# A scaled sum split into three pieces: early x quarters of an attention and MoE kernel

## The chip, the cores and the metric

The kernel runs on one core of one Trainium2 chip. The metric is the device time of one execution in microseconds (us). TensorE is called PE, VectorE DVE, ScalarE ACT, GpSimd POOL; SP only issues DMAs here. Each engine works through its own list of instructions in order and waits on semaphores for the others.

## The reference

Attention with a learned bias of relative positions, and after it a feed-forward pair of products whose input is the attention's output.

```
scores = scale * q @ k^T                       # batch 4, heads 8, seq 576, head_dim 64
x = (log1p(|i - j|) / log1p(max(i, 1)))[..., None]
scores += relu(x @ w1 + b1) @ w2               # a bias for every head
attn = exp(scores - max);  attn /= sum + 1e-9
a = attn @ v                                   # as 2304 tokens x 512
h = a @ w_in                                   # 512 x 2048
g = h where h >= 1, 0 where h <= -1, else (h + 1)^2 / 4
out = g @ w_out                                # 2048 x 512
```

## The kernel before, in words

Every fp32 product is made of products of numbers that are split into a high and a low part. So beside each product there are splits: a cast to the high part, and a subtraction for the low part.

There are three stages. Up to some 69 us the bias of all heads is computed and stored to DRAM. From there to some 345 us runs the attention, in 16 units n = 0 to 15 (a pair of heads and a batch each, some 17 us a unit). Then comes the feed-forward part (MoE).

A unit has five blocks of rows, k = 0 to 3 and L. A block makes two PSUM tiles of scores `S{n}_{k}_{j}` on PE (lines 455 and 456; the L block one tile, 476 and 477). DVE adds the bias, writes the result to SBUF as `e` and finds the row's extreme `mx` in one instruction (458, for L 478). ACT takes the exponential (465, 484). PE transposes `e` into PSUM tiles `T` (521, 526, 535), and these are split into `hi` and `lo` on ACT and DVE (496, 497), or by way of an ACT copy `c` (501) on DVE (505) or POOL (503) for `hi` and POOL (506) for `lo`. Then come the products with v on PE (559, 561), whose PSUM tiles `O` ACT copies out (562). They are stored to DRAM as `xT`, not yet divided by the sums of the rows; the reciprocals of these sums are stored as `rT`. PSUM has two buffers for all `S` tiles of the stage, so a score tile can start only when the tile two before it has been read by DVE: `S_3_1` waits for the read of `S_2_1`, `S_L` for the read of `S_3_0`.

For the next units the same engines cast k (163) and v (178) on DVE and make their low parts on POOL (136).

The MoE needs the attention's output as x, in quarters (k, j) of 128 x 384, multiplied by the reciprocals and split. Eight of these quarters, j = 0 and 1 of block 0, are made in the attention already, as soon as their tokens are complete. `load_x` asks for two halves of `xT` and for the reciprocals, and `split_x` (399) hands back three pieces: `scaled` (DVE: `scale_x`, the sum of the two halves at 396 and the product with the reciprocals at 397, each 128 x 384), `high` (ACT, 409) and `rest` (POOL, 413). `plan_x` (593) puts the load into half-step T and piece i into half-step T1 + i of a table `XQ`; a half-step is half a block, ten to a unit, so T1 = 43 is unit 4, half-step 3. The early quarters (0,0), (1,0) and (2,0) fall into units 4, 8 and 12; the other five into units 13 to 15. The home of a quarter is a buffer of another use: "raw" is also that of the next weights' load.

The order on an engine is partly pinned: what goes through `keep` stays in the program's order, the rest is placed by a scheduler when the kernel is built. The MoE makes its later x with `scale_x` itself.

Of the kernel before, what the change touches and what calls it, by code (L numbers as in the profile page):

```python
# [13 lines left out]
ALU = mybir.AluOpType  # L14
# [33 lines left out]
def attn_cpb_moe_kernel(ctx, tc, qk, vL, cb, win, wout, lw, ident, ii, out):  # L48
    nc = tc.nc
# [6 lines left out]
    TH = TB // 2  # L56
# [81 lines left out]
    def keep(ins):  # L138
        tc.keep_in_program_order(ins)

    def pool(ins):
        if KEEP and go[0]:
            tc.keep_in_program_order(ins)
# [213 lines left out]
    def x_tile(z, k, part, name):  # L357
        if z == 0:
            return xp0.tile([P, TH], F32R, tag=f"x{'hl'[part]}{k}", name=name)
        at = 2 * k + part  # L360
        g = min(at // 3, 2) + (at == 7)
        if at % 3 == 0 or at == 7:
            tag, w, n_ = ("qk", QW, CFG["rawb"][0]) if g < 2 else ("v", 10 * D, CFG["rawb"][1])
            room[g] = lp.tile([P, w], F32R, tag=tag, name=name, bufs=n_)
        c0 = TH * (at % 3 if at < 6 else 0)
        return room[g][:, c0 : c0 + TH]

    def load_x(blk, k, j, home="x"):

        src = xT[k][blk // TB][:, :, TH * j : TH * j + TH].rearrange("(s d) i c -> d s i c", s=2)  # L370
        rp = rps[0]
        if home != "raw":
            if home == "bias":
                r = bp.tile([P, 2 * S], F32, tag="bias", name=f"x{blk}_{k}_{j}").rearrange("p (a b) -> p a b", a=3)
            else:
                r = rp.tile([P, 3, TH], F32, tag="x", name=f"x{blk}_{k}_{j}", bufs=1)
            r, rr = r[:, 0:2], r[:, 2]
        else:
            r = rp.tile([P, 2 * DM], F32, tag="raw", name=f"x{blk}_{k}_{j}")[:, : 2 * TH].rearrange("p (a b) -> p a b", a=2)
            rr = rp.tile([P, DM], F32, tag="a", name=f"xr{blk}_{k}_{j}")[:, :TH]  # L380
        for i in range(2):
            nc.sync.dma_start(out=r[D * i : D * i + D], in_=src[:, :, i])
        c0 = blk + TH * j
        c1 = c0
        while c1 < c0 + TH:
            t = c1 % S
            e = min(c0 + TH, c1 - t + (512 if t < 512 else S))
            for i in range(2):
                at = 512 * i + t if t < 512 else 1024 + D * i + t - 512
                row = rT[k][c1 // S][at : at + e - c1].unsqueeze(0)  # L390
                nc.sync.dma_start(out=rr[D * i : D * i + D, c1 - c0 : e - c0], in_=row.to_broadcast((D, e - c1)))
            c1 = e
        return r, rr

    def scale_x(r, rr, out):
        keep(nc.vector.tensor_tensor(out=r[:, 0], in0=r[:, 0], in1=r[:, 1], op=ALU.add))
        keep(nc.vector.tensor_tensor(out=out, in0=r[:, 0], in1=rr, op=ALU.mult))

    def split_x(k, j, home):

        r, rr = load_x(0, k, j, home)
        x = r[:, 0]

        def scaled():
            scale_x(r, rr, x)

        def high():
            xs[k, j] = [x_tile(j, k, i, f"x{'hl'[i]}0_{k}_{j}") for i in range(2)]
            keep(nc.scalar.copy(xs[k, j][0], x))

        def rest():
            h, l = xs[k, j]
            pool(nc.gpsimd.tensor_tensor(out=l, in0=x, in1=h.bitcast(F32), op=ALU.subtract))

        return scaled, high, rest

    with ExitStack() as ph:
        tp1 = ph.enter_context(tc.tile_pool(name="a_eT1", bufs=1))
# [172 lines left out]
        def plan(T, f):  # L591
            jobs.setdefault(T, []).append(f)

        def plan_x(k, j):
            T, home, T1 = XQ[k, j]

            def load():
                assert all((k, t) in made for t in range(TH * j, TH * j + TH))
                for i, f in enumerate(split_x(k, j, home)):
                    plan(T1 + i, f)  # L600

            plan(T, load)
# [96 lines left out]
    with ExitStack() as ph:  # L699
# [232 lines left out]
        for blk in (0, TB):  # L932
            for m in range(2 * NF):
                f, j = m // 2, m % 2
# [4 lines left out]
                c = gp.tile([P, TH], F32, tag="c", name=f"c{blk}_{m}")  # L939
# [47 lines left out]
        for g in range(NG2):  # L987
            blk, f = b2, 2 * g
            for s_ in range(NS):
# [31 lines left out]
                else:  # L1021
                    fo, j = {2: (f, 0), 4: (f + 1, 1), 5: (f + 1, 0), 6: (f, 1)}[s_]
# [78 lines left out]
```

## Time and profile before

| | |
|---|---|
| time, median of 3 runs | 747.65 us (746.45 to 749.12) |
| the profiled execution's own time | 747.49 us |
| its span, first to last instruction | 745.7 us |
| PE busy | 701.6 us, 94% of the span |
| DVE, POOL, ACT busy | 541.5, 519.2, 516.4 us |
| mean granted PE clock | 0.992 |

The span is the stretch that the trace covers; the remaining 1.8 us lie around it. Busy shares are means over three stages that differ: what one place is worth is read in the rows of that place. A duration in the timeline can hold time in which an instruction had begun and was held up.

### The profile page before, as it was taken

To read this page: it belongs to the slowest core of one execution; us is meant where nothing else is said; L and a number is where in the kernel's file an instruction comes from. 1 tells how busy PE (TensorE), PEld (TensorE's weight loads), DVE (VectorE), ACT (ScalarE), POOL (GpSimd) and SP (SyncE) were. 2 spreads that over 40 slices of the span, in tenths; PEclk is the share of its full clock that TensorE was granted. 3 is DMA by queue.
4 is the path that set the end of the run, shared out by engine and by line. 5 is a ranking of instruction groups with operands and counts; after the bars stand their busy time and mean duration, and the time that the engine had idled before them with its cause. 6 is when DMAs were issued, how large, how long until landed. Compare 5 with 4: busy or idle time off the path is not lost. (4 is left out here: it accounts for less than half of the span.)

```text
span 745.7 us, 13716 instructions
## 1 busy us (share of the span) xinstructions
PE 701.6 (94%) x4640; PEld 620.3 (83%) x4640; DVE 541.5 (73%) x1047; ACT 516.4 (69%) x1151; POOL 519.2 (70%) x440
## 2 busy tenths in 40 slices
PE   5687999999999999999999999999999998999997
PEld 2234899998988889889988898898989987888896
DVE  7899888888898898886876866354465557666653
ACT  8896989888888889877565656444534446666563
POOL 8986777888878888852667677466655645666652
PEclk9999999999999999999999999999999999999999
DMA  8887799977997898634355554133021002000002
GB/s 231 239 268 227 200 250 244 305 204 183 263 234 196 201 256 205 156 113 147 113 177 162 189 155 138 43 96 75 1 65 32 1 4 82 1 1 1 0 1 85
DMA packets 58518, 103.37 MB, mean 139 GB/s; under 512 B 12480, under 2 KB 32464, under 8 KB 58448
## 3 DMA queue, kind: packets, MB, share of 16 engines
q1 hardware_dynamic: 56000, 92.44, 43.7%
q0 software_dynamic: 2304, 9.96, 6.4%
q8 instruction: 37, 0.61, 0.4%
q14 instruction: 33, 0.27, 0.1%
q10 hardware_dynamic: 144, 0.09, 0.1%
HBM read 67.38 MB, written 25.12 MB: 124 GB/s over the span
## 5 line engine op out<-in xcount | busy, mean ns | idle before, releaser
L951 POOL TENSOR_TENSOR gl<-c,gh 128x384 fp32r<-128x384 f32 x64 | 70.9, 1107 | 104.2 <-issue 86.8
L506 POOL TENSOR_TENSOR lo<-c,hi 128x512 fp32r<-128x512 f32 x75 | 101.5, 1369 | 29.7 <-DVE hi L505 27.1
L716 PE MATMUL y<-w1h,gl 128*128 128x512 f32 x288 | 114.0, 396 | 0.0
L716 PE MATMUL y<-w1l,gh 128*128 128x512 f32 x288 | 113.7, 395 | 0.0
L716 PE MATMUL y<-w1h,gh 128*128 128x512 f32 x288 | 112.0, 389 | 0.0
L465 ACT ACTIVATE e<-e,mx 128x576 f32<-128x576 f32 x128 | 100.6, 790 | 12.7 <-DVE mx L458 12.6
L458 DVE CUSTOM_DVE_ANT_0 e<-S,bias 128x576 f32<-128x576 f32 x128 | 94.3, 750 | 12.6 <-PE S L456 12.0
L455 PE MATMUL S<-kh,qa 128*128 128x288 f32 x256 | 78.4, 323 | 6.8 <-DVE mx L458 4.6
L769 ACT ACTIVATE c<-c,half_s 128x384 f32<-128x384 f32 x64 | 39.4, 616 | 60.7 <-DVE c L766 60.7
L456 PE MATMUL S<-ls,qa 128*128 128x288 f32 x256 | 72.3, 300 | 0.0
L521 PE MATMUL T<-id_s,e 128*128 128x128 f32 x512 | 70.7, 274 | 1.3 <-DVE lo L497 0.8
L977 POOL TENSOR_TENSOR gl<-c,gh 128x384 fp32r<-128x384 f32 x32 | 32.8, 1024 | 50.0 <-issue 23.3
L716 PEld LDWEIGHTS y<-w1h,gl 128*128 128x128 f32 x288 | 54.0, 187 | 11.6
L521 PEld LDWEIGHTS T<-id_s,e 128*128 128x128 f32 x512 | 58.7, 142 | 4.1 <-DVE lo L497 1.3
L284 ACT ACTIVATE u<-lw,nthr 128x576 f16<-128x576 f32 (+17 forms) x104 | 57.7, 644 | 5.1 <-PE B L303 2.7
L716 PEld LDWEIGHTS y<-w1l,gh 128*128 128x128 f32 x288 | 54.0, 187 | 8.0
L716 PEld LDWEIGHTS y<-w1h,gh 128*128 128x128 f32 x288 | 54.1, 188 | 7.7
L303 PEld LDWEIGHTS <-qh 128*32 128x32 f16 x704 | 19.1, 102 | 49.2 <-issue 21.2
L455 PEld LDWEIGHTS S<-kh,qa 128*128 128x128 f32 x256 | 48.2, 188 | 11.7 <-DVE mx L458 8.7
L772 DVE TENSOR_TENSOR c<-h,c 128x384 f32<-128x384 f32 x64 | 35.5, 554 | 26.8 <-ACT c L769 26.0
L286 POOL TENSOR_SCALAR u<-lw,thr 128x576 f16<-128x576 f32 (+17 forms) x36 | 51.5, 1442 | 4.3 <-PE B L303 3.1
L947 ACT CAST gh<-c 128x384 fp32r<-128x384 f32 x64 | 32.9, 513 | 30.7 <-DVE c L772 28.7
(264 smaller groups left out, 2117.5 us busy)
## 6 DMA issues: line engine op xcount, KB each, us to landing
bias_d<-y SPq DMA_DIRECT2D x36, 295.5 KB
qk<-in_qk_dram SPq DMA_DIRECT2D x16, 608.0 KB
qa<-in_qk_dram POOLq DMA_DIRECT2D x16, 608.0 KB, 7.0
x<-xT SPq DMA_DIRECT2D x48, 192.0 KB
raw<-in_win_dram SPq DMA_DIRECT2D x16, 512.0 KB
raw<-in_wout_dram SPq DMA_DIRECT2D x16, 512.0 KB
v<-in_vL_dram SPq DMA_DIRECT2D x16, 320.0 KB
qa<-ls SPq DMA_DIRECT2D x32, 152.0 KB
```

Source lines behind the costliest of these rows:

```text
L284: tc.keep_in_program_order(nc.scalar.activation(u[:, :n_], lw1[:, :n_], AF.Sigmoid, bias=nthr[:, m : m + 1], scale=STEEP))
L286: EN[x].tensor_scalar(out=u[:, :n_], in0=lw1[:, :n_], scalar1=thr[:, m : m + 1], scalar2=None, op0=ALU.is_gt)
L455: nc.tensor.matmul(ps[:, hf, :HS], qs[:, qc], kh[:, kc : kc + HS], start=True, stop=False)
L456: nc.tensor.matmul(ps[:, hf, :HS], q0[:, qc], kl[:, kc : kc + HS], start=False, stop=True)
L458: nc.vector.tensor_tensor_reduce(out=ev.rearrange("p (a b) -> p a b", a=2), in0=ps[:, :, :HS], in1=bias[k][:, S * j : S * j + S].rearrange ...
L465: lambda ev=ev, j=j: nc.scalar.activation(ev, ev, AF.Exp, bias=mx[:, j : j + 1], scale=-1.0, accum_out=sm[:, 4 * j + k : 4 * j + k + 1])
L506: r = nc.gpsimd.tensor_tensor(out=lo, in0=m, in1=hi.bitcast(F32), op=ALU.subtract)
L521: nc.tensor.transpose(ps[:, tb, :], e[:, c0 : c0 + P], id_s)
L716: a = nc.tensor.matmul(out, w, x, start=start, stop=stop)
L769: keep(nc.scalar.activation(c, c, AF.Square, scale=0.5, bias=half_s))
L772: keep(nc.vector.tensor_tensor(out=c, in0=h, in1=c, op=ALU.max))
L951: keep(nc.gpsimd.tensor_tensor(out=gl, in0=c, in1=gh.bitcast(F32), op=ALU.subtract))
```

## The change

The pieces of a quarter become five: the sum, the first half of the product (columns 0 to 191), its second half (192 to 383), the high part, the low part. For the quarters (0,0), (1,0) and (2,0) they stand in half-steps T1, T1 + 1, T1 + 2, T1 + 2, T1 + 3, in place of T1 (sum and product), T1 + 1, T1 + 2. For the other five the sum and both halves stay together in T1, and high and low part keep their half-steps.

```
-        def scaled():
-            scale_x(r, rr, x)
+        def summed():
+            keep(nc.vector.tensor_tensor(out=x, in0=x, in1=r[:, 1], op=ALU.add))
+
+        def scaled(i):
+            c = slice(TH // 2 * i, TH // 2 * i + TH // 2)
+            keep(nc.vector.tensor_tensor(out=x[:, c], in0=x[:, c], in1=rr[:, c], op=ALU.mult))
...
-        return scaled, high, rest
+        return summed, lambda: scaled(0), lambda: scaled(1), high, rest
...
-                for i, f in enumerate(split_x(k, j, home)):
+                for i, f in zip((0, 1, 2, 2, 3) if j == 0 and k < 3 else (0, 0, 0, 1, 2), split_x(k, j, home)):
                     plan(T1 + i, f)
```

What this does to the lists of the engines is shown at three places. First DVE in unit 4, before; x0_0_0 is the quarter, xr0_0_0 its reciprocals, vs5 the next unit's v, and the ISA rows are the reads of score tiles (e, mx):

```order
L396 TENSOR_TENSOR x0_0_0_2469<-x0_0_0_2469 128x384
L397 TENSOR_TENSOR x0_0_0_2469<-x0_0_0_2469,xr0_0_0_2470 128x384
L178 CAST vs5_2696<-v5_2515 128x10x64
L458 ISA e4_2_2609,mx4_2_2608<-S4_2_1_2616,bias1_2_2361 128x576
L458 ISA mx4_2_2608 128x1
L497 TENSOR_TENSOR lo4_0_2557<-T4_1_0_2627,hi4_0_2556 128x4x128
L497 TENSOR_TENSOR lo4_0_2557<-T4_1_1_2634,hi4_0_2556 128x4x128
L458 ISA e4_3_2649,mx4_3_2648<-S4_3_0_2650,bias1_3_2400 128x576
L458 ISA mx4_3_2648 128x1
L497 TENSOR_TENSOR lo4_0_2557<-T4_s0_2641,hi4_0_2556 128x256
L458 ISA e4_3_2649,mx4_3_2648<-S4_3_1_2656,bias1_3_2400 128x576
```

and now:

```order
L405 TENSOR_TENSOR x0_0_0_2469<-x0_0_0_2469 128x384
L178 CAST vs5_2697<-v5_2515 128x10x64
L462 ISA e4_2_2608,mx4_2_2607<-S4_2_1_2615,bias1_2_2361 128x576
L462 ISA mx4_2_2607 128x1
L409 TENSOR_TENSOR x0_0_0_2469<-x0_0_0_2469,xr0_0_0_2470 128x192
L501 TENSOR_TENSOR lo4_0_2557<-T4_1_0_2624,hi4_0_2556 128x4x128
L501 TENSOR_TENSOR lo4_0_2557<-T4_1_1_2631,hi4_0_2556 128x4x128
L462 ISA e4_3_2649,mx4_3_2648<-S4_3_0_2650,bias1_3_2400 128x576
L462 ISA mx4_3_2648 128x1
L501 TENSOR_TENSOR lo4_0_2557<-T4_s0_2638,hi4_0_2556 128x256
L409 TENSOR_TENSOR x0_0_0_2469<-x0_0_0_2469,xr0_0_0_2470 128x192
L462 ISA e4_3_2649,mx4_3_2648<-S4_3_1_2656,bias1_3_2400 128x576
```

The product has left the place between the sum and the cast of v; its first half stands behind the read of S4_2_1, its second half behind `lo` of T4_s0, ahead of the read of S4_3_1. Units 8 and 12 change in the same way.

Then ACT in the same unit, before; xh0_0_0 is the quarter's high part, c a copy of a transposed tile, x4_0 the copies of the products with v:

```order
L465 ACTIVATE e4_2_2609,sum4_2476<-e4_2_2609,mx4_2_2608 128x576
L409 CAST xh0_0_0_2624<-x0_0_0_2469 128x384
L496 CAST hi4_0_2556<-T4_s0_2641 128x256
L501 COPY c4_2669<-T4_2_0_2664 128x512
L501 COPY c4_2678<-T4_2_1_2673 128x512
L465 ACTIVATE e4_3_2649,sum4_2476<-e4_3_2649,mx4_3_2648 128x576 x2
L562 COPY x4_0_2698<-O4_0_0_2699 128x256
L484 ACTIVATE e4_L_2685,sum4_2476<-e4_L_2685,mx4_4_2684 128x576
L562 COPY x4_0_2698<-O4_0_1_2711 128x256
```

and now:

```order
L469 ACTIVATE e4_2_2608,sum4_2476<-e4_2_2608,mx4_2_2607 128x576
L500 CAST hi4_0_2556<-T4_s0_2638 128x256
L505 COPY c4_2670<-T4_2_0_2665 128x512
L505 COPY c4_2679<-T4_2_1_2674 128x512
L469 ACTIVATE e4_3_2649,sum4_2476<-e4_3_2649,mx4_3_2648 128x576
L413 CAST xh0_0_0_2645<-x0_0_0_2469 128x384
L469 ACTIVATE e4_3_2649,sum4_2476<-e4_3_2649,mx4_3_2648 128x576
L566 COPY x4_0_2699<-O4_0_0_2700 128x256
L566 COPY x4_0_2699<-O4_0_1_2712 128x256
L488 ACTIVATE e4_L_2686,sum4_2476<-e4_L_2686,mx4_4_2685 128x576
```

The high part of the quarter goes behind the first exponential of block 3, and the exponential of the L block goes behind the second copy x4_0. POOL's list is the same as before, so its low part of the quarter stands ahead of the same instructions as before.

Last DVE at quarter (3,0), in unit 14, before; lo13_1 are low parts of the unit before:

```order
L505 CAST hi13_1_4995<-T13_3_1_5105 128x4x128
L396 TENSOR_TENSOR x0_3_0_5017<-x0_3_0_5017 128x384
L497 TENSOR_TENSOR lo13_1_4996<-T13_L_5143,hi13_1_4995 128x4x64
L397 TENSOR_TENSOR x0_3_0_5017<-x0_3_0_5017 128x384
L497 TENSOR_TENSOR lo13_1_4996<-T13_s1_5152,hi13_1_4995 128x320
```

and now:

```order
L509 CAST hi13_1_4999<-T13_3_1_5109 128x4x128
L405 TENSOR_TENSOR x0_3_0_5021<-x0_3_0_5021 128x384
L501 TENSOR_TENSOR lo13_1_5000<-T13_L_5148,hi13_1_4999 128x4x64
L409 TENSOR_TENSOR x0_3_0_5021<-x0_3_0_5021 128x192 x2
L501 TENSOR_TENSOR lo13_1_5000<-T13_s1_5157,hi13_1_4999 128x320
```

One product has become two instructions next to each other, with nothing else moved. It is the same at (0,1), (1,1), (2,1) and (3,1).

## Rows read from the trace of the kernel before

**Rows 1.** Windows, 140 to 300 us: PE, PEld, DVE, ACT, POOL busy; clock, DMA

```profile
140.00:300.00 160.00, 150.95 (x1151) 143.23 (x1150) 140.84 (x305) 140.66 (x366) 132.52 (x110) 1.00 0.88 223
```

**Rows 2.** Timeline of PE: start, duration, line, operation, idle before it, its releaser

```profile
142.60 0.40 PE L455 MATMUL S<-kh,qa 128*128 128x288 f32 x1 [1.16 <-DVE mx L458]
211.86 0.40 PE L455 MATMUL S<-kh,qa 128*128 128x288 f32 x1 [1.54 <-DVE mx L458]
279.84 0.40 PE L455 MATMUL S<-kh,qa 128*128 128x288 f32 x1 [1.04 <-DVE mx L458]
```

**Rows 3.** Timeline of DVE in unit 12

```profile
276.56 1.73 DVE L397 TENSOR_TENSOR x<-x,xr 128x384 f32<-128x384 f32 x1
278.21 0.90 DVE L178 CAST vs<-v 128x640 fp32r<-128x640 f32 x1
279.03 0.74 DVE L458 CUSTOM_DVE_ANT_0 e<-S,bias 128x576 f32<-128x576 f32 x1
279.70 1.28 DVE L497 TENSOR_TENSOR lo<-T,hi 128x512 fp32r<-128x512 f32 x2
```

**Rows 4.** Timeline of POOL in unit 12

```profile
274.61 3.26 POOL L136 TENSOR_TENSOR ls<-qk,kh 128x608 fp32r<-128x608 f32 x2
277.81 0.95 POOL L503 CAST hi<-c 128x512 fp32r<-128x512 f32 x1
278.84 1.40 POOL L506 TENSOR_TENSOR lo<-c,hi 128x512 fp32r<-128x512 f32 x1
```

**Rows 5.** Timelines of DVE and POOL, instructions that no other one blocked

```profile
595.72 0.42 DVE L866 TENSOR_TENSOR sum_w<-sum_w,w 128x256 f32<-128x256 f32 x1
299.61 0.54 DVE L397 TENSOR_TENSOR x<-x 128x384 f32<-128x384 f32 x1
295.61 1.28 POOL L506 TENSOR_TENSOR lo<-c,hi 128x512 fp32r<-128x512 f32 x1
```

**Rows 6.** Timelines of DVE, POOL and PE at quarter (2,1), unit 15

```profile
324.25 1.64 DVE L397 TENSOR_TENSOR x<-x 128x384 f32<-128x384 f32 x1
324.20 1.28 POOL L506 TENSOR_TENSOR lo<-c,hi 128x512 fp32r<-128x512 f32 x1
326.77 0.82 PE L559 MATMUL O<-hi,vs 128*128 128x320 f32 x4 [1.59 <-DVE sum L672]
```

**Rows 7.** Timeline of PE in unit 12, start of S_L

```profile
281.71 0.40 PE L476 MATMUL S_L<-kh,qa 128*128 128x288 f32 x1
```

**Rows 8.** Timelines of DVE and POOL in unit 8

```profile
208.79 0.85 DVE L397 TENSOR_TENSOR x<-x,xr 128x384 f32<-128x384 f32 x1
211.73 1.28 DVE L497 TENSOR_TENSOR lo<-T,hi 128x512 fp32r<-128x512 f32 x2
209.31 1.48 POOL L506 TENSOR_TENSOR lo<-c,hi 128x512 fp32r<-128x512 f32 x1
```

**Rows 9.** Timelines of ACT and DVE behind unit 8: e_L, T_L

```profile
216.60 0.78 ACT L484 ACTIVATE e_L<-e_L,mx 128x576 f32<-128x576 f32 x1
221.19 0.37 ACT L496 CAST hi<-T_L 128x256 fp32r<-128x256 f32 x1
221.84 0.42 DVE L497 TENSOR_TENSOR lo<-T_L,hi 128x256 fp32r<-128x256 f32 x1
```

**Rows 10.** Timelines of DVE and POOL at quarter (0,1), unit 13

```profile
301.82 0.76 DVE L458 CUSTOM_DVE_ANT_0 e<-S,bias 128x576 f32<-128x576 f32 x1 [0.40 <-PE S L456]
299.76 1.55 POOL L506 TENSOR_TENSOR lo<-c,hi 128x512 fp32r<-128x512 f32 x1 [2.87 <-DVE hi L505]
```

**Rows 11.** Timelines of DVE, POOL and PE at quarter (3,0), unit 14

```profile
307.00 0.63 DVE L397 TENSOR_TENSOR x<-x 128x384 f32<-128x384 f32 x1
307.29 2.75 POOL L506 TENSOR_TENSOR lo<-c,hi 128x512 fp32r<-128x512 f32 x2
308.17 0.82 PE L559 MATMUL O<-hi,vs 128*128 128x320 f32 x4 [0.92 <-DVE lo L497]
```

**Rows 12.** Busy time and granted clock behind the wait at 326.77

```profile
329.00:331.00 2.00, 2.00 (x10) 2.00 (x9) 0.57 (x1) 1.94 (x5) 0.00 (x0) 0.50 0.70 198
```

## The prediction

> **What bounds the kernel now.** I read the page's busy shares first, then windows of the attention, then PE's waits there, and last the timelines of DVE, POOL and PE side by side around each early quarter. In the middle of the attention PE works 150.95 of 160 us, but DVE 140.84, ACT 140.66 and POOL 132.52 [rows 1]: PE is ahead by little, and what keeps it waiting is a chain on DVE here and there. Three of its longest waits there stand at the same place, `S_3_1` in units 4, 8 and 12, released by `mx`, the read of `S_2_1`: 1.16 + 1.54 + 1.04 = 3.74 us [rows 2]. That is all that the spreading of the first three quarters can win directly.
>
> Unit 12 shows why the read is late. The product begins at 276.56 and lasts 1.73 us [rows 3], where one that nothing blocks takes 0.54 [rows 5]. It ends at 278.29, that is 0.42 behind the end of POOL's pair `ls` (274.61 + 3.26 = 277.87) [rows 4]. The cast `vs` begins at 278.21 and ends at 279.11, 0.35 behind the end of POOL's `hi` (277.81 + 0.95 = 278.76); and POOL's next, `lo`, begun at 278.84, ends at 280.24, 1.13 behind the end of `vs` [rows 3, 4]. So a DVE instruction that takes all its operands from SBUF and a POOL instruction exclude each other. They take turns, one whole instruction each, although on DVE's list product and `vs` are neighbours. The read of `S_2_1` (279.03) waits behind both.
>
> **Prices.** A product of 384 columns costs 0.54, a DVE sum of 256 columns 0.42 [rows 5], so 0.001 a column, and a half of 192 some 0.36 us when free. Behind a block it needs 0.42 - 0.18 = 0.24 from the release. If POOL has an instruction ready when the first of two neighbouring halves ends, the second half waits for it: 1.13 for a `lo`. Two halves then end 0.24 + 1.13 + 0.24 - 0.42 = 1.19 us later than one product.
>
> The row shows `hi` between product and `vs` (278.29 to 278.76) although both DVE instructions were ready [rows 3, 4]. The Trainium skill ("SBUF — State Buffer", section "SBUF: two separate sides") says of the pair of ports that DVE and GpSimd share that it is "an exclusive lock, not a bandwidth split", held for the whole instruction. By that rule every added instruction boundary gives POOL one more turn, which speaks against cutting a product in two; if a lock outlasted the boundary, the two halves would cost about what the product does. The trace agrees with the page.
>
> **Units 4, 8 and 12.** In unit 12 the sum stays as it is. `vs` follows it and waits for the pair `ls` until 277.87, so it ends at 278.22, 0.89 before 279.11; the read of `S_2_1` starts at 278.14 and `S_3_1` at 279.84 - 0.89 = 278.95. Most of its wait goes. What is late next is `S_L`, which needs the read of `S_3_0`, and that stands on DVE behind first half, `lo`, `lo`. Before, it started at 281.71 [rows 7].
>
> The first half starts 0.67 behind the read (279.03 to 279.70 in [rows 3]), at 278.81. POOL, freed by `vs` at 278.22, makes `hi` (0.47, as 278.29 to 278.76) and starts `lo` 0.08 later, at 278.76 or 278.77 [rows 4]. The two ask for the port within 0.05 us. The trace has this very race at quarter (2,1): POOL's `lo` started at 324.20, DVE's product at 324.25, and the product took 1.64 and ended 0.41 behind `lo`'s end at 325.48 [rows 6]. POOL won. So I take it that POOL wins here too. Its `lo` runs 1.28 [rows 5] to 280.04, the half ends at 280.28, and the pair `lo` of DVE starts at 280.20 where it started at 279.70 [rows 3]: **+0.50**, and `S_L` with it. Should DVE win, the half ends at 279.17 and the pair starts at 279.09: -0.61. Unit 4 has the same wait but for 0.12 us [rows 2]: I take +0.50 and -0.61 there too.
>
> Unit 8 is other: there the product ended at 209.64, POOL's `lo`, begun at 209.31, took the port from it and ended at 210.79 [rows 8], and `vs` had to wait for that. Now `vs` takes the product's place, ends at 209.57 (release at 209.64 - 0.42 = 209.22, and 0.35), and `lo` ends 1.13 later at 210.70. The first half waits for that, ends at 210.94, and DVE's pair starts at 210.86 where it started at 211.73 [rows 8]: **-0.87**. Sum of the three: +0.13 (or -2.09 if DVE wins both races).
>
> The second half lies between `lo` and the read of `S_3_1`, while POOL waits for this quarter's high part: 0.28 more on DVE, covered by PE's products with v between `S_L` and the next unit. High and low part come some 2 us later; POOL has 27 of 160 us free [rows 1] and nobody in the attention waits for them, only the next load into "raw". If that cover were gone, POOL's lateness would price at most one `lo`, 1.28, a unit.
>
> **ACT.** `e_L`'s exponential, which ran from 216.60 while ACT waited for the second product with v [rows 9], now stands behind the second copy. ACT is later by at most these 0.78. `hi` of `T_L` started at 221.19, took 0.37, and DVE read it at 221.84: 0.28 of slack [rows 9]. The bounds are 0 and 0.78 - 0.28 = 0.5 a unit for the products with v that need these low parts; ACT's gaps and its later copies, now ahead of an exponential, bring it near the slack, so I take 0.3, three times: **+0.9**.
>
> **The other five quarters.** (1,1) and (3,1): POOL waits for DVE or ACT at that time, so nothing stands between the halves: 0.06 each, hidden. (0,1): the product started at 299.61 and POOL's `lo` at 299.76, blocked by it (1.55 against 1.28) [rows 5, 10]. The first half would end at 299.97, `lo` takes the port, and the second half is 1.19 late; DVE's wait for PE at 301.82 covers 0.40 [rows 10]: **+0.79**. (3,0): the product ended at 307.63 with POOL's `lo` waiting since 307.29 [rows 11]. The first half ends at 307.45, `lo` goes next, and DVE's low part behind the second half is the one that PE already waits 0.92 us for [rows 11]: **+1.19**, nothing covers it. (2,1): the first half ends at 325.48 + 0.24 = 325.72, POOL's second `lo` is ready, and PE waits 1.59 us for what DVE does next [rows 6]: **+1.19**.
>
> **Sum.** 0.13 + 0.9 + 0.79 + 1.19 + 1.19 = +4.2 us, against a profiled execution of 747.49 us: 751.7. That execution lies 0.16 below the median, so 751.8 us.
>
> **Rivals.**
> 1. *DVE wins the races by some hundredths.* For it: they are decided by 0.05 us, and small shifts reach each of them. Then units 4, 8 and 12 bring -2.09; at (3,0) the halves pass before POOL (0.06), but at (0,1) POOL is ready 0.11 before the second half and at (2,1) its second `lo` waits anyway: -2.09 + 0.9 + 0.79 + 0.06 + 1.19 = +0.85, 748.5 us. Partly so, by one race, about 750.
> 2. *The halves pass as one and the waits of [rows 2] go.* For it: the two halves do not depend on each other, as sum and product do. Against it: product and `vs` don't either, and POOL came between. It would give -2.09, at best the whole -3.74: 743.9 to 745.6 us, faster.
> 3. *The clock falls.* Behind the wait of 1.59 us the granted clock was 0.50, the lower level, 1.2 GHz [rows 12], so each 2 us there held the work of 1. The wait before (2,1)'s products grows to 2.8 us, and at (3,0) from 0.92 to 2.1. If the clock falls at (3,0) too, where it did not before, that costs 1 to 2 us more: 753 to 754 us. The point of decision is whether PE's wait there passes the 1.59 us that did bring it down at 326.77. Against it: 1.54 us in unit 8 is almost the same, and the clock was full over the whole stretch [rows 1].
> 4. *It doesn't do what it says:* POOL's place against DVE drifts so far in the later units that no half of the last five is cut off: +0.13 + 0.9, again about 748.7 us.
>
> **How the numbers follow.** What a measurement of this kernel can tell from no change is about 0.3%, 2.2 us: 745.4 to 749.9. My forecast 0.40 (749 to 753, three quarters of it above 749.9), rival 1 0.20, rival 2 0.10, rival 3 0.18, rival 4 0.12. Faster: rival 2 but for its weak end, 0.08. Same: rivals 1 and 4, a quarter of the forecast, and the rest of rival 2: 0.44. Slower: three quarters of the forecast and rival 3, 0.48. The range leaves out rival 2 and the tail of rival 3: 746.5 to 754.5.
>
> **What would show it.** Right: the waits at `S_3_1` in units 4, 8, 12 shrink to 0.3 us or less, waits of about 1 us appear at `S_L` of the same units, and a half of 192 columns that should take 0.36 lasts 1.3 to 1.6 us at (0,1), (3,0) and (2,1), with a POOL `lo` ending 0.24 before it; PE's waits now at 308.17 and 326.77 grow by over 1 us. Wrong: the first halves in units 4 and 12 last 0.36 and `S_L` starts at once (rival 1); or the last five quarters' halves all last 0.36 (rivals 2 and 4); or ACT's later `e_L` shows no wait behind it, then 0.9 of the sum is gone; or a granted clock of 0.50 at (3,0) (rival 3).

## The result, and the profile after

The changed kernel takes 753.5 us (median of 4 runs, 753.26 to 753.85), the kernel before took 747.39 us beside it (746.45 to 749.12). The ratio is 1.007, 95% interval 1.0045 to 1.0095: slower by about 5.2 us. (The ratio is estimated from all the runs; it is not the quotient of the two medians, which is 1.008.) The forecast was 751.8 us in a range of 746.5 to 754.5.

| | before | after |
|---|---|---|
| profiled execution's own time | 747.49 us | 753.41 us |
| its span | 745.7 us | 751.6 us |
| PE, DVE, ACT, POOL busy | 701.6, 541.5, 516.4, 519.2 us | 704.2, 546.4, 517.2, 517.8 us |
| mean granted PE clock | 0.992 | 0.989 |

The busy times hardly tell the two apart; the middle of the attention looks as in [rows 1]. The windows of 140 to 300 us after (us, PE, PEld, DVE, ACT, POOL busy, granted clock, DMA share, GB/s):

```profile
140.00:300.00 160.00, 151.09 (x1134) 141.43 (x1133) 142.17 (x302) 139.33 (x361) 132.53 (x110) 1.00 0.85 222
```

The difference lies in waits, so I compare the times at which PE reaches the same instruction in both traces: the first matmul of `S_L` and the transpose `R` that ends a unit. The table gives after minus before.

| at PE's | difference | step since the row above |
|---|---|---|
| `S_L` of unit 0 | +1.51 us | +1.51, ahead of all that changed |
| `R` of unit 3 | +1.47 | 0 |
| `S_L` of unit 4 | +1.97 | +0.50 |
| `S_L` of unit 5 | +2.73 | **+0.76** |
| `R` of unit 7 | +1.79 | -0.94 |
| `S_L` of unit 8 | +1.94 | +0.15 |
| `S_L` of unit 9 | +2.67 | **+0.73** |
| `R` of unit 11 | +3.22 | +0.55 |
| `S_L` of unit 12 | +3.03 | -0.19 |
| `S_L` of unit 13 | +3.73 | **+0.70** |
| `R` of unit 13 | +5.56 | +1.83 |
| `S_L` of unit 14 | +5.26 | -0.30 |
| `R` of unit 14 | +6.28 | +1.02 |

Three of these steps I don't count to the change. The first 1.51 us arise before the lists of the engines differ. The -0.94 is a wait of PE for a DMA `kh<-kh`, 0.98 us long at 199.43 in the trace of before and missing after; of the +0.55, 0.31 is the same wait ahead of unit 12 (0.23 before, 0.54 after). The last section has more on both. The other steps are +0.46 at the three `S_L`, +2.19 behind them and +2.55 at the late quarters: 5.2 us. That this meets the ratio so well is partly luck: the +0.15 and the -0.19 begin behind those DMA waits and depend on them, and the low clock behind quarter (2,1) is in both traces, though not in every execution of the kernel before (last section).

**The waits that the change was to move.** PE at `S_3_1` in units 4, 8 and 12, answering [rows 2] (start, duration, line, operation, idle before it, releaser):

```profile
143.20 0.40 PE L459 MATMUL S<-kh,qa 128*128 128x288 f32 x1 [0.29 <-DVE mx L462]
212.42 0.40 PE L459 MATMUL S<-kh,qa 128*128 128x288 f32 x1 [0.32 <-DVE mx L462]
282.18 0.40 PE L459 MATMUL S<-kh,qa 128*128 128x288 f32 x1 [0.17 <-DVE mx L462]
```

3.74 us of waits have become 0.78. In units 4 and 8 another comes a few instructions later: PE's transposes wait 0.84 us for the low parts that stand on DVE behind the first half (unit 4):

```profile
145.26 0.63 PE L525 MATMUL T<-id_s,e 128*128 128x128 f32 x4 [0.84 <-DVE lo L501]
```

DVE and POOL in units 4, 8 and 12:

```profile
143.07 1.45 DVE L409 TENSOR_TENSOR x<-x,xr 128x192 f32<-128x192 f32 x1
143.02 1.28 POOL L510 TENSOR_TENSOR lo<-c,hi 128x512 fp32r<-128x512 f32 x1
212.29 1.45 DVE L409 TENSOR_TENSOR x<-x,xr 128x192 f32<-128x192 f32 x1
212.25 1.28 POOL L510 TENSOR_TENSOR lo<-c,hi 128x512 fp32r<-128x512 f32 x1
282.05 0.76 DVE L409 TENSOR_TENSOR x<-x,xr 128x192 f32<-128x192 f32 x1
281.18 1.42 POOL L510 TENSOR_TENSOR lo<-c,hi 128x512 fp32r<-128x512 f32 x1
```

In units 4 and 8 POOL's `lo` starts 0.04 or 0.05 us ahead of the half and goes first; a half that should cost 0.36 ends 0.21 or 0.22 behind the end of `lo`. In unit 12 `lo` had begun 0.87 earlier, and the half loses only what is left of it; experiment 2 shows that this place depends on the execution.

**Behind unit 4.** POOL, DVE and PE on the way to `S_L` of unit 5, after (five rows) and POOL and DVE before (two rows):

```profile
147.84 1.02 POOL L417 TENSOR_TENSOR xl<-x,xh 128x384 fp32r<-128x384 f32 x1 [3.53 <-ACT xh L413]
157.20 2.98 POOL L136 TENSOR_TENSOR ls<-qk,kh 128x608 fp32r<-128x608 f32 x2
159.05 1.48 DVE L178 CAST vs<-v 128x640 fp32r<-128x640 f32 x1 [0.97 <-PE O L565]
161.26 0.40 PE L459 MATMUL S<-kh,qa 128*128 128x288 f32 x1 [0.38 <-DVE mx L462]
163.65 0.40 PE L480 MATMUL S_L<-kh,qa 128*128 128x288 f32 x1 [1.16 <-DVE mx L462]
...
154.49 2.96 POOL L136 TENSOR_TENSOR ls<-qk,kh 128x608 fp32r<-128x608 f32 x2
156.74 1.07 DVE L178 CAST vs<-v 128x640 fp32r<-128x640 f32 x1 [1.08 <-PE O L561]
```

POOL stands idle for 3.53 us until the quarter's high part is there, and only then makes the low part, with its full list behind it. Its pair `ls` starts 2.71 us later than before (154.49), though PE had come only 1.5 to 2.0 us late. DVE's `vs` starts 2.31 us later than before, meets the second `ls` and lasts 1.48 (1.07 before); the read of a score tile behind it is 2.72 us later than before, and PE waits 0.38 us at `S_3_1` of unit 5, where it did not before. `S_L` of unit 5 is 2.73 us later: POOL's delay has come through to PE whole.

**The late quarters.** DVE, POOL and PE at (0,1), (3,0) and (2,1), answering [rows 10, 11, 6] (DVE's row at (0,1) is the second half alone, the others are both halves):

```profile
303.61 1.45 DVE L409 TENSOR_TENSOR x<-x 128x192 f32<-128x192 f32 x1
303.50 1.34 POOL L510 TENSOR_TENSOR lo<-c,hi 128x512 fp32r<-128x512 f32 x1 [2.87 <-DVE hi L509]
306.38 0.40 PE L459 MATMUL S<-kh,qa 128*128 128x288 f32 x1 [0.54 <-DVE mx L482]
...
311.42 1.76 DVE L409 TENSOR_TENSOR x<-x 128x192 f32<-128x192 f32 x2
311.71 2.61 POOL L510 TENSOR_TENSOR lo<-c,hi 128x512 fp32r<-128x512 f32 x2
313.73 0.82 PE L563 MATMUL O<-hi,vs 128*128 128x320 f32 x4 [2.17 <-DVE lo L501]
...
329.44 2.78 DVE L409 TENSOR_TENSOR x<-x 128x192 f32<-128x192 f32 x2
329.39 2.62 POOL L510 TENSOR_TENSOR lo<-c,hi 128x512 fp32r<-128x512 f32 x2
333.10 1.41 PE L563 MATMUL O<-hi,vs 128*128 128x320 f32 x4 [2.73 <-DVE sum L676]
```

Each time a POOL `lo` stands between the two halves, and PE's waits grow from 0.92 to 2.17 and from 1.59 to 2.73 us. The granted clock behind the wait of 2.17 us stayed at 1.00; behind that of 2.73 it fell to 0.50, the lower level, as behind the 1.59 us before [rows 12]:

```profile
314.00:316.00 2.00, 2.00 (x15) 2.00 (x14) 1.86 (x6) 1.40 (x4) 2.00 (x3) 1.00 1.12 171
334.00:336.00 2.00, 2.00 (x9) 2.00 (x9) 1.90 (x5) 0.77 (x2) 0.00 (x0) 0.50 0.29 78
```

### The profile page after: what moved, and what is told of

It reads as the page before. It is cut to its first block, busy times and chain, and to the rows that moved or that the text cites. A ratio compares the mean times of both kernels' runs of the same rounds, so it can differ in the third digit from the quotient of the medians.

```text
span 751.6 us, 13725 instructions
## 1 busy us (share of the span) xinstructions
PE 704.2 (94%) x4640; PEld 622.0 (83%) x4640; DVE 546.4 (73%) x1055; ACT 517.2 (69%) x1151; POOL 517.8 (69%) x440
## 4 chain that ended last, share of the span: by engine, by line
PE 69%; DVE 7%; ACT 6%; issue 3%; DMA 3%; SPq 1%; POOL 1%; ACTq 0%; DVEq 0%; POOLq 0%
PE y L720 24%; PE h L720 16%; PE O L563 8%; PE p L720 7%; PE T L525 4%; PE S L459 3%; PE S L460 2%; PE O L565 2%; ACT e L469 2%; DVE x L409 1%; DVE e L462 1%; PE S_L L480 1%; ACT c L505 1%; DVE lo L501 1%; DMA xT<-x 1%
## 5 line engine op out<-in xcount | busy, mean ns | idle before, releaser
L563 PE MATMUL O<-hi,vs 128*128 128x256 f32 (+1 forms) x256 | 48.8, 308 | 5.4 <-DVE sum L676 2.7
```

The source lines that it names most:

```text
L563: nc.tensor.matmul(ps[:, :w], vs[:, 4 * j + tb, :], src[:, 4 * j + tb, :], start=first and tb == 0, stop=False)
```

## The experiments

Ten runs on three occasions; those of one occasion share the runs of the kernel before. `whole` stands for the undivided product, `split_x` handing back four pieces then.

**1. The late halves alone.** The early three quarters get the whole product back in the half-steps of before:

```
-return summed, lambda: scaled(0), lambda: scaled(1), high, rest
+return (summed, whole, high, rest) if j == 0 and k < 3 else (summed, lambda: scaled(0), lambda: scaled(1), high, rest)
...
-zip((0, 1, 2, 2, 3) if j == 0 and k < 3 else (0, 0, 0, 1, 2), ...)
+zip((0, 0, 1, 2) if j == 0 and k < 3 else (0, 0, 0, 1, 2), ...)
```

> The kernel before with one change: the product of the five later quarters in two neighbouring halves; units 4, 8 and 12 as before. Theory A (DVE and POOL take turns, one whole instruction each, so a half is held for a POOL lo at (0,1), (3,0) and (2,1)): second halves of 1.3 to 1.6 us at these three, 0.3 at (1,1) and (3,1); PE's wait now at 308.17 grows from 0.92 to about 2.1 and that at 326.77 from 1.59 to about 2.7; +2.5 to +3 us against before, all of it between S_L of unit 13 and the end of the attention. Rival B (a half costs only its own fixed time): all halves 0.36, at most +0.3 us.

Measured: 752.77 against 747.78 us, ratio 1.0054 (1.0033 to 1.0074). PE's waits at the three places:

```profile
301.53 0.40 PE L462 MATMUL S<-kh,qa 128*128 128x288 f32 x1 [0.54 <-DVE mx L485]
308.89 0.82 PE L566 MATMUL O<-hi,vs 128*128 128x320 f32 x4 [2.12 <-DVE lo L504]
328.24 1.41 PE L566 MATMUL O<-hi,vs 128*128 128x320 f32 x4 [2.73 <-DVE sum L679]
```

From `S_L` of unit 13 to the end of the attention the trace loses 2.55 us against before, as in the changed kernel. Cutting these products in two, with no other instruction moved, costs 0.0054 of the change's 0.007 by the timed runs (4.0 us, interval 2.5 to 5.5), but only about half of it by the pair of traces; the clock behind (2,1) can make the difference (last section). Rival 2, that the halves pass as one, falls.

**2. The early quarters alone.** The reverse: the early three as changed, the late five with `whole` in half-steps 0, 0, 1, 2.

> The changed kernel with the product of the five later quarters whole again; the first three quarters stay spread in halves. Theory A: S_L of units 4, 8, 12 moves by +0.5, +0.15, -0.2 against the S_L before them as in the changed kernel, each unit behind them loses 0.7 more, the DMA wait ahead of unit 8 gives back 0.9: some +2 us against before, 2.5 to 3 less than the changed kernel. Rival B (all of the loss sits in units 4, 8, 12): +5 us against before, as the changed kernel.

Measured: 749.04 against 747.78 us, ratio 1.0017 (1.0001 to 1.0033). Up to unit 13 its trace loses about what the changed kernel loses (+0.50 and +0.74 in unit 4, for instance), and nothing behind. The two excesses, 0.0054 and 0.0017, add up to the change's 0.007. Unit 12 came out otherwise than in the changed kernel's trace, where PE had waited 0.54 us for a DMA just before. Here there was no such wait, POOL's `lo` won by 0.05 us again, and the half met the whole of it (DVE and POOL in unit 12):

```profile
281.57 1.45 DVE L409 TENSOR_TENSOR x<-x,xr 128x192 f32<-128x192 f32 x1
281.52 1.28 POOL L513 TENSOR_TENSOR lo<-c,hi 128x512 fp32r<-128x512 f32 x1
```

From `S_L` of unit 11 to that of unit 12 this trace and that of experiment 4 lose 0.50 us against before, the changed kernel's 0.36. The expected -0.2 was a reading of that one execution.

**3. Only ACT's exponential later.** The kernel before, with `e_L`'s exponential of units 4, 8 and 12 behind the second copy, as the changed kernel has it:

```
+copies[n, half] = nc.scalar.copy(x[:, j, :w], ps[:, :w])
...
+with ExitStack() as after:
+    if n in (4, 8, 12):
+        after.enter_context(tc.issue_after(copies[n, 0].ins))
     y = nc.scalar.activation(e, e, AF.Exp, bias=mx[:, 0:1], ...)
```

> The kernel before with one change: in units 4, 8 and 12 ACT takes the exponential of the L block behind the second copy of the product with v, as the changed kernel's list has it. Theory A (ACT's lateness holds up PE's transposes of the next unit's first block): +0.35 us in each of units 5, 9, 13, +1.0 in all. If ACT alone makes the whole loss of 0.7 behind each of these units: +2.2. Rival (POOL's later low part makes it, ACT has slack): 0.

Measured: 748.86 against 747.78 us, ratio 1.0002 (0.9985 to 1.0019). At `R` of units 4, 8 and 12 PE is 0.44 us later, so the delay is there; but at the next `S_L` it has been given back to within 0.1 us, since PE's wait there shrinks from 1.16 to 0.96 us and the other waits on the way with it:

```profile
161.80 0.41 PE L476 MATMUL S_L<-kh,qa 128*128 128x288 f32 x1 [0.96 <-DVE mx L458]
```

**4. The changed kernel with that exponential early.** The other way round: in the changed kernel `e_L`'s exponential goes ahead of the second copy again (the copy under `issue_after` of the exponential).

> The changed kernel with the exponential of the L block ahead of the second copy again in units 4, 8 and 12. Theory A: the 0.35 us that transposes wait in units 5, 9 and 13 go, about -1.0 us against the changed kernel, while the 0.4 that the next S_3_1 waits behind a late vs stay. If ACT alone makes the loss: -2.2. Rival (POOL alone): 0.

Measured: 752.76 against 747.78 us, ratio 1.0061 (1.0044 to 1.0077). PE reaches `R` of unit 4 with no loss since `S_L`, but `S_L` of unit 5 is 0.74 us late all the same: the wait moves to `S_3_1`, 0.71 instead of 0.38.

```profile
161.56 0.41 PE L459 MATMUL S<-kh,qa 128*128 128x288 f32 x1 [0.71 <-DVE mx L462]
163.95 0.40 PE L480 MATMUL S_L<-kh,qa 128*128 128x288 f32 x1 [1.15 <-DVE mx L462]
```

So the place of `e_L`'s exponential is not what costs 0.7 us behind each unit. What experiments 2 and 4 and the changed kernel share is the quarter's high part, late on ACT, and POOL's low part, which waits for it.

**5. The whole product in the first half's place.** Half-steps 0, 1, 1, 2 for sum, `whole`, high and low part of the early three; late five whole.

> The three early quarters have the whole product where the changed kernel has its first half, and high and low part right behind it, so that POOL's low part falls into its idle gap ahead of the transposes of block 2 again; the other five quarters have whole products as before. Theory P (the 0.7 us lost behind each of units 4, 8 and 12 in the changed kernel are POOL's lateness: its low part of the quarter waits for the second half and then stands in front of full work): the loss behind the unit is gone. What is left is the product's blocking by POOL's lo, which is 0.18 longer for 384 than for 192 columns: S_L of unit 4 +0.67, of unit 8 +0.33, of unit 12 0.0 against the kernel before, sum +1.0, ratio 1.001. Theory Q (the loss behind the unit comes from the later S_L, or from the place of the product on DVE, whatever POOL does): +0.7 behind each unit stays, sum +3.1, ratio 1.004.

Measured: 749.15 against 749.34 us, ratio 1.0000 (0.9978 to 1.0021). POOL's low part of unit 4 and DVE's product before it, and PE's first matmul behind unit 4:

```profile
143.30 1.65 DVE L412 TENSOR_TENSOR x<-x,xr 128x384 f32<-128x384 f32 x1
145.57 1.01 POOL L420 TENSOR_TENSOR xl<-x,xh 128x384 fp32r<-128x384 f32 x1 [1.04 <-ACT xh L416]
151.50 0.37 PE L462 MATMUL S<-kh,qa 128*128 128x288 f32 x1 [1.40 <-DMA kh<-kh]
```

The low part lies in POOL's gap. `S_L` of unit 4 comes 0.69 us later than in the kernel before (0.67 expected). Behind units 8 and 12 the loss is -0.01 us each time, where the changed kernel has +0.73 and +0.70. That is theory P. Unit 4 doesn't show it: there PE waited 1.40 us for a DMA `kh<-kh`, and 1.06 us were lost. `S_L` of unit 12 was a miss: 0.67 us later since `S_L` of unit 11, where 0.0 was expected, because here too the product met the whole `lo`. Unit 8 can't be read (last section).

**6. The whole product in the second half's place.** Half-steps 0, 2, 2, 3 for the early three; late five whole.

> The three early quarters have the whole product where the changed kernel has its second half, ahead of the read of S_3_1; high and low part in the changed kernel's places; the other five quarters have whole products as before. Theory P (POOL's late low part costs 0.7 behind each unit): no DVE instruction stands between the read of S_2_1 and the two low parts, so PE's waits of 0.84 and 0.17 ahead of S_L go, and S_L is 0.5, 0.85 and 0.5 us earlier than in the kernel before (units 4, 8, 12), sum -1.9; behind each unit +0.7 is lost as in the changed kernel, sum +2.1; in all +0.2, ratio 1.000. Theory Q (the loss behind the unit comes from the later S_L): nothing is lost behind, in all -1.9, ratio 0.9975.

Measured: 747.36 against 749.34 us, ratio 0.9983 (0.9962 to 1.0004). `S_L` of unit 4 comes 0.87 us earlier than in the kernel before (0.5 expected), that of unit 12 0.33 us (0.5 expected), but behind units 4, 8 and 12 the loss is 1.11, 1.10 and 1.09 us: with PE and DVE earlier, a low part that still waits for ACT is later against them (PE's `S_L` of unit 4, and POOL's low part):

```profile
145.38 0.40 PE L483 MATMUL S_L<-kh,qa 128*128 128x288 f32 x1
147.14 1.02 POOL L420 TENSOR_TENSOR xl<-x,xh 128x384 fp32r<-128x384 f32 x1 [2.53 <-ACT xh L416]
```

Theory Q, which had nothing lost behind an early `S_L`, falls. The three losses were larger than I had written (0.7). Another 1.5 us went in unit 5 of this execution, where the granted clock fell behind waits of 0.65 and 1.16 us (1.00 over the same part of unit 5 in the kernel before):

```profile
164.00:168.00 4.00, 4.00 (x26) 3.98 (x25) 3.21 (x7) 1.66 (x4) 2.30 (x3) 0.71 0.73 270
```

**7. Two late products moved.** The kernel before, with the products of (3,0) and (2,1) two half-steps later, and their high and low parts one. (The expectation has the high parts two later and the low parts as before; the edit puts 0, 2, 2, 3 in place of 0, 0, 1, 2. In the traces POOL's low parts and ACT's high part of (3,0) keep their places among the instructions around them.)

```
+zip((0, 2, 2, 3) if (k, j) in ((3, 0), (2, 1)) else (0, 0, 1, 2), ...)
```

> The kernel before, with the products of the quarters (3,0) and (2,1) and their high parts two half-steps later (behind the low parts that PE waits for); sums, low parts and all other quarters as before. Theory A (the product on DVE in front of the low part, and the turn of POOL that it lets in, is what PE waits for at these two places): the wait of 0.92 us at (3,0) falls by 0.55, the wait of 1.59 us at (2,1) by about 1.4 (DVE's low part then starts when ACT's high part is there, at about 324.2), and a granted clock of 0.50 behind it, where there was one, does not come: -2.0 without and -3.4 us with the clock, less some 0.5 us for the product in its new place: ratio 0.996 to 0.998. Rival: the waits stay, because ACT's or POOL's part of the chain ends as late, or the products meet POOL in their new places and lose there what they won: ratio 0.999 to 1.002.

Measured: 745.97 against 749.34 us, ratio 0.9959 (0.9938 to 0.9981): faster than before. The wait at (3,0) is 0.35 (0.37 expected), that at (2,1) is gone (some 0.2 expected), and the clock behind it is full (PE at (3,0); then a window behind (2,1)):

```profile
309.72 0.82 PE L566 MATMUL O<-hi,vs 128*128 128x320 f32 x4 [0.35 <-DVE lo L504]
```

```profile
328.00:330.00 2.00, 2.00 (x16) 2.00 (x15) 2.00 (x5) 1.97 (x6) 0.93 (x1) 1.00 0.00 2
```

From `S_L` of unit 13 to `R` of unit 14 the trace gains 3.0 us on the profiled kernel before, about 1.5 of it by the clock; 2.6 are left at the first matmul of the MoE.

**8. POOL's low part later, and a change in the MoE.** The kernel before, with the early quarters' low part (`rest`) at T1 + 4 instead of T1 + 2; on POOL it then stands behind the two `lo` of block 2. The edit has a second line, which the expectation doesn't mention: in the MoE, of every seven low parts of one kind, the fourth goes to POOL and the fifth to DVE, the other way round than before:

```
-en = nc.vector if i % NS in (0, 1, 3) else nc.gpsimd
+en = nc.vector if i % NS in (0, 1, 4) else nc.gpsimd
```

> The kernel before; only POOL's low part of the three early quarters stands behind its two lo of block 2 in units 4, 8 and 12, instead of ahead of them, where POOL waited anyway. Nothing else moves in the attention. In all runs so far the next unit's S_L starts 6.42 us (behind units 4 and 8) or 5.90 us (behind unit 12) after POOL's pair ls, in every kernel. Theory P (POOL's list up to ls paces the unit, so 1.02 us more in front of ls is 1.02 us more in the unit): S_L of units 5, 9 and 13 about +1.0 us each, though S_L of units 4, 8 and 12 and all of DVE's and ACT's lists are unchanged; sum +3.1, ratio 1.004, and the distances 6.42, 6.42 and 5.90 stay. Theory Q (POOL's low part has cover, as the prediction had it, and the loss behind the units came from the product's place): no change, ratio 1.000, and the distances shrink by what POOL is later.

Measured: 745.48 against 748.51 us, ratio 0.9978 (0.9955 to 1.0001). This ratio says nothing about POOL's low part, since the MoE was changed with it: from `R` of unit 15 to the end this trace takes 398.8 us, the other eleven 400.2 to 402.4. The attention's trace can be read. Theory P expected +1.0 us at each of the next `S_L` and was wrong here. POOL's `ls` did come 0.98 us later against PE, but `S_L` of unit 5 came 0.41 us *earlier*, which was gone again by the end of unit 5. POOL and DVE there, and PE's `S_L`:

```profile
156.67 3.22 POOL L136 TENSOR_TENSOR ls<-qk,kh 128x608 fp32r<-128x608 f32 x2
158.02 0.51 DVE L178 CAST vs<-v 128x640 fp32r<-128x640 f32 x1 [1.15 <-PE O L561]
159.87 1.12 DVE L116 SCALAR_TENSOR_TENSOR a<-a,raw 128x512 int32<-128x512 int32 x1 [0.66 <-ACT a L112]
161.72 0.41 PE L476 MATMUL S_L<-kh,qa 128*128 128x288 f32 x1 [0.89 <-DVE mx L458]
```

With POOL this late, DVE asks for `vs` when the first `ls` is ending, takes the turn between the two (0.51 us, where it took 1.07 before and 1.48 after), and the next SBUF instruction `a` meets a short cast and not a `lo`. Theory Q's reason, cover, is not right either: the distance from `ls` to `S_L`, which was 6.41 to 6.45 us behind units 4 and 8 in all nine profiled executions before this one, is 5.05 here because the turns fall otherwise. How little decides it, experiment 4 shows: there `vs` came at 159.03, the second `ls` had begun at 159.00, and `vs` had to wait for all of it (1.81 us). Over the whole attention up to `S_L` of unit 13 this trace gains 0.11 us on that of before, where theory P had it lose 3.1.

**9 and 10. A combination, and experiment 7 again.** Experiment 6's early quarters, with ACT's high part ahead of the first exponential of block 3 (that exponential under `issue_after` of the high part), and experiment 7's two moved products.

> Three early quarters with the whole product ahead of the read of S_3_1, high and low part in the changed kernel's places, and ACT making the high part ahead of the first exponential of block 3 in units 4, 8 and 12; the products of (3,0) and (2,1) two half-steps later; the other quarters as before. Theory P: with the high part some 0.5 us earlier, POOL's low part ends some 0.6 us earlier and the loss behind the three units is about 0.45 instead of 1.1 us, with S_L ahead by 0.9, 0.7 and 0.4 as in the run with the product at the second half's place: -0.2 to -0.5 a unit, some -1 us in all; with the -2 to -3 us of the two moved products -3 to -4 us against the kernel before, ratio 0.9945 to 0.996. Theory Q (POOL's low part is not what costs the 1.1): 1.1 stays behind each unit, ratio 0.997.

> The kernel before with only the products of (3,0) and (2,1) two half-steps later, run again beside the combination: 0.996 as the first time. If it equals the combination, the early quarters' new places bring nothing.

Measured: the combination 744.93 against 748.51 us, ratio 0.9965 (0.9943 to 0.9986); experiment 7's kernel again 745.59 us, ratio 0.9975 (0.9957 to 0.9993). The loss behind units 4, 8 and 12 of the combination is 0.59, 0.72 and 0.69 instead of 1.1 us: the earlier high part gave 0.4 to 0.5 back, as theory P had it, but more is left than the 0.45 I expected. The two ratios can't be told apart, so what the early quarters' new places add to the two moved products is too small to be shown. Both kernels beat the kernel before, and so the changed one.

## Why the prediction came out as it did

**Right, and shown: a cut product costs a turn of POOL.** The late quarters were to cost 3.17 us; the trace has 2.55, experiment 1 a ratio of 1.0054 by itself. (0,1) and (3,0) together cost 1.83 of 1.98, (2,1) 1.02 of 1.19; 0.30 came back at `S_L` of unit 14, whose wait of 0.27 us in the kernel before is gone. The near match with 2.55 leaves out the clock: the prediction took it as low behind (2,1) before and after, as in its trace, but whole products lost it in two executions of six, cut ones in three of three (last section). The halves lasted what the price said: 1.45 where a `lo` of 1.28 came first. The Trainium skill ("SBUF — State Buffer", section "SBUF: two separate sides") has the port pair as an exclusive lock held for a whole instruction; the trace agrees, with halves that end 0.21 or 0.22 us behind the end of the POOL instruction.

**Right: units 4 and 12.** Unit 4: +0.50 of +0.50. In unit 12 of the changed kernel's trace POOL's `lo` had started 0.87 us ahead of the half and not with it, and the table has -0.19, a step that begins behind a DMA wait. From `S_L` of unit 11 it is +0.36, and where no such wait came before it (experiments 2 and 4) +0.50 both times. The waits came elsewhere than the sign that I had named: 0.84 us at the transposes and only 0.17 at `S_L`.

**Wrong in size: unit 8.** Forecast -0.87, measured +0.15. I let `vs` take the product's place against POOL as it was in [rows 8], so that POOL's `lo` would be over when the half came. In the trace its `lo` starts at 212.25, and the half meets the whole of it, as in unit 4. [rows 8] were no good base: the profiled kernel before had waited 0.98 us for a DMA ahead of unit 8. In experiments 1 and 3, with the same lists there and without that wait, product and `vs` meet POOL as in unit 4, and against them the changed kernel's step from `S_L` of unit 7 is +0.46 and +0.48.

**Wrong: the term for ACT.** The step "+0.9" for `e_L`'s exponential did not hold. The exponential does delay `R` by 0.44 us (experiment 3), but the next unit gives it back, and putting it early again wins nothing (experiment 4).

**Wrong: POOL's later low part at no cost.** The step was "nobody in the attention waits for them". True of the low part itself; what stands *behind* it on POOL is waited for. (The prediction bounded this case at 1.28 us a unit; 0.70 to 0.76 came.) POOL had 27 of 160 us free, but the low part left the gap in which it had lain (it began at 143.93 in unit 4 before) and stood in front of a list without gaps up to `ls`. That cost 2.19 us in the three units. Experiment 5 shows it for two of them (low part back in the gap, loss gone), and the loss follows the low part: in unit 4 it began 1.40 us behind `S_L` in the changed kernel, 1.77 in experiment 6 and 1.37 in experiment 9, and 0.76, 1.11 and 0.59 us were lost. Experiments 3 and 4 exclude the place of `e_L`'s exponential. They do not exclude ACT's late high part, which moved with the low part in all these runs; that the loss goes by way of POOL is read from the trace behind unit 4, where POOL's delay of 2.71 us reaches `S_L` whole. It is no plain sum of lateness, though: in experiment 8, the only one that moved POOL's low part alone in the attention, POOL was late by 0.98 us and nothing was lost, since the turns between POOL and DVE fell in DVE's favour. That reading of experiment 8 is argued from its rows; no run forced the turns one way and the other.

So that the total came near is partly luck: 4.2 us forecast against 5.2 measured, with 0.9 too much at ACT and 2.2 too little at POOL, and the lateness behind the three units was no term of the sum. The end of the range was chosen for rival 3, the clock at (3,0), which did not come: the wait there grew to 2.17 us and the clock stayed full.

## What to carry to other kernels

Where two engines exclude each other by whole instructions, count boundaries: a cut that adds no work still gives the other engine one more turn, and it costs that engine's instruction, here 1.2 us. When work moves later on an engine, its idle share doesn't tell what that costs (POOL had 27 of 160 us free here); look whether it leaves a gap and what stands behind it on that engine up to the next thing that someone waits for. And an instruction that excludes another engine was better put behind the result that the critical engine waits for than divided: two such moves gained 0.25 to 0.4%, where the cuts lost 0.5%.

## What the runs showed that was not expected

**The clock behind the same wait differs between executions.** Behind (2,1)'s wait the granted clock fell to 0.50 in the profiled kernel before and in experiment 6 (wait 1.59 us in both), but not in experiments 2, 3, 5 and 8 (1.59 to 1.60). With the product cut (the changed kernel, experiments 1 and 4) the wait was 2.73 us and the clock fell in all three. PE behind the wait in experiment 2, then the window behind it, then that of experiment 6:

```profile
330.70 0.83 PE L566 MATMUL O<-hi,vs 128*128 128x320 f32 x4 [1.59 <-DVE sum L679]
```

```profile
332.00:334.00 2.00, 2.00 (x16) 1.94 (x15) 1.51 (x4) 1.93 (x5) 0.00 (x0) 1.00 0.31 59
...
331.00:333.00 2.00, 2.00 (x10) 2.00 (x9) 1.83 (x4) 0.77 (x3) 0.25 (x1) 0.50 0.19 29
```

It is worth some 1.5 us: from `S_L` to `R` of unit 14 experiment 2 takes 1.5 us less than the kernel before, with the same waits. So the late cuts cost more than the pair of traces shows whenever the whole product would have kept the clock: from `S_L` of unit 13 to `R` of unit 14 the changed kernel takes 4.1 us more than experiment 2, which is what experiment 1 was timed at (4.0 us). A single profiled execution is no better than that at this place; the timed ratios decide.

**The start of the attention, too.** From 70 to 74 us the granted clock was 0.57 in the changed kernel's profiled execution and 1.00 in that of before, with the same instructions:

```profile
70.00:74.00 4.00, 3.96 (x16) 3.45 (x16) 3.00 (x7) 1.68 (x4) 0.00 (x0) 0.57 0.99 298
```

```profile
70.00:74.00 4.00, 3.35 (x21) 2.64 (x20) 3.58 (x11) 1.63 (x4) 0.00 (x0) 1.00 0.98 294
```

Experiments 1, 3 and 10 had 1.00, the others 0.57 to 0.60; `S_L` of unit 0 came at 77.59 to 78.51 us with the one and at 78.86 to 79.44 with the other.

**The wait for the DMA `kh<-kh`** came and went likewise: 0.98 us ahead of unit 8 in the kernel before, none at that place in experiment 1, whose lists are the same up to unit 13, and up to 1.59 us in experiment 9. Each of the three is worth 1 to 1.5 us, so, as an estimate, a single pair of traces of this kernel can differ by some 3 us without any change.

**The step into unit 8** is as unsteady. From `S_L` of unit 7 to that of unit 8, five executions with the same lists in between (the kernel before, experiments 1, 3, 7 and 10) differ from the first of them by 0, -1.24, -1.26, +0.87 and -1.21 us; those with the changed lists (the changed kernel, experiments 2 and 4) by -0.78, -0.79 and -0.87. In experiment 7 there was no such DMA wait, but PE waited 1.84 us for `mx` at `S_3_1` of unit 8 and the granted clock behind it fell to 0.50. Against the three that agree the change costs 0.3 to 0.5 us there; the pair of traces alone can't price it.
